# RWKV-6 attention with a channel MLP: how w, k and r of rounds 3 to 7 come to stand with their channels on the partitions

## The chip, the cores and the metric

One NeuronCore of one Trainium2 chip. The time is the device time of one execution in microseconds. The kernel before was run three times: 587.10, 587.24 and 587.42 us, median 587.24. One further execution was recorded by the hardware profiler. It took 585.66 us, of which 583.9 lie between its first and its last instruction (the span); it is a little faster than the median of the others, by 1.6 us.

## What is computed

The reference in two stages. The first is a recurrence over 768 time steps for each of 4 batches and 8 heads, with a head dimension D of 48:

```python
for t in range(S):
    cur = einsum('bhd,bhe->bhde', u * k[t], v[t])
    y[t] = einsum('bhd,bhde->bhe', r[t], state + cur)
    state = w[t][..., None] * state + einsum('bhd,bhe->bhde', k[t], v[t])
```

The second takes the heads side by side as 384 channels, normalizes each step over its channels, scales with `g_ln`, multiplies by `w_ch1` (384 x 1536), takes the positive part, multiplies by `w_ch2` (1536 x 384) and adds the input. Everything is float32.

## The kernel before, in words

**Units and rounds.** A unit is one batch, one half of the sequence (RN = 384 steps) and four heads (two pairs); a round is two units, numbered `g`, so there are 8 rounds of 2 units, `q` = 0 to 15. In the code's main loop (L821) `rnd` is the round whose attention is worked on (`now`), `old` is the one before it and `new` the one after it. While `now` goes through its six levels (`lev` 0 to 5), the MLP of an older round fills TensorE, `old` gets its states and outputs, and the inputs of `new` are loaded and turned.

**The levels.** The attention within chunks of 64 steps is built by doubling: at each level TensorE computes quadrants of scores from k and r (`quads`, L411, into the PSUM tile a_ps), VectorE multiplies k and r by products of w (`grow`, L431) and puts the new scores into the matrix A (`keep`, L448). `grow` of a level comes after `quads` of that level, and `quads` of the next level needs it. After level 5, k is turned back (`ends`, L485, PSUM tile kn_ps), and in levels 0 and 1 of the next round `states` (L504) multiplies it with v (kv) and VectorE runs ten steps of state update; in levels 2 and 3 `outputs` (L560) gives y, which VectorE adds up into x. At level 3 `moments` and `norm` (L597, L607) make the normalized xn on VectorE; at level 4 TensorE turns it (`turned_x`, L623, tile xT_ps); from level 5 on the MLP of that round (`mlp`, L635) runs in steps of three matmuls with 384 columns each (h_ps, then o_ps).

**Turning.** `grow` and `quads` need w, k and r with the channels on the partitions (two heads at 0 and 64) and the steps along the free dimension; in memory the 48 channels of a step lie together. Before, `load` (L122) brings a tensor of a unit with three DMAs of 128 steps x 4 heads x 48 floats into `nat_w`, `nat_k`, `nat_r` (two buffers each, by `q % 2`), steps on the partitions, and `turned` (L306) takes a pair of heads: three TensorE transposes of 128x128 into one PSUM tile (w_ps, k_ps or r_ps) and one ScalarE copy into `wT` or `rkT`. The natural k and r are also what `own_products` (L358, on GpSimd) reads for the term of a step with itself.

**What sets the order.** The compute engines are wrapped so that their instructions stay in the program's order (`InOrder`, L39). In each level the loop collects `tasks` and `fill` (L692) puts them between steps of the MLP. Loads and stores go through the SP queue; its instructions are placed by the framework's scheduler. An instruction on SP waits for the buffer that it writes, and for the completion of the DMA eight places ahead of it, since eight semaphores are used in turn; what stands behind it on SP waits too.

**Weights.** The MLP weights are read early, in 24 pieces of 128 x 768 words, through the tag `raw` of the pool `p4`, which has four buffers; the last piece is used up in round 1's levels.

The part of the loop that the change touches, L866 to L881 of the kernel before, says at which level w, k and r of `new` are loaded and turned: in round 2 w is turned at level 3 and k and r of the two units at levels 4 and 5; in later rounds at levels 1, 2 and 3.

Of the kernel before, what the change touches and what calls it, by code (L numbers as in the profile page):

```python
# [9 lines left out]
F32 = mybir.dt.float32  # L10
# [42 lines left out]
def kernel(  # L53
# [13 lines left out]
    PE, ACT, DVE, POOL, SPO = (  # L67
        InOrder(tc, e) for e in (nc.tensor, nc.scalar, nc.vector, nc.gpsimd, nc.sync)
    )
    SP = nc.sync  # L70

    B, H, S, D = r.shape
    P = 128
    HP = 64
    C = 64
    NH = 4
    NP = NH // 2
    U = H // NH
    TT = 3
    RN = TT * P  # L80
# [3 lines left out]
    W = NK * P  # L84
# [6 lines left out]
    pairs = range(NP)  # L91
# [3 lines left out]
    p1 = ctx.enter_context(tc.tile_pool(name="p1", bufs=1))  # L95
    p2 = ctx.enter_context(tc.tile_pool(name="p2", bufs=2))
    p3 = ctx.enter_context(tc.tile_pool(name="p3", bufs=3))
    p4 = ctx.enter_context(tc.tile_pool(name="p4", bufs=4))
# [8 lines left out]
    units = [(b, f, g) for b, f in rounds for g in range(U)]  # L107
    NU = len(units)
# [24 lines left out]
    def load_rows(nm, q, eng):  # L133

        b, f, g = units[q]
        src = {"w": w, "k": k, "r": r}[nm]
        eng.dma_start(
            out=flat(nm, q)[:, 0 : NH * TT * D].rearrange("p (h x) -> p h x", h=NH),
            in_=src[b, ts(g, NH), ds(f * RN, RN)].rearrange("h (p c) d -> p h (c d)", c=TT),
        )  # L140

    def load_v(q, eng=SP):
        vn[q] = p4.tile([P, TT, NH, D], F32, tag="v", name=f"v{q}")
# [21 lines left out]
    for j in range(2):  # L165
        ACT.dma_start(
            out=sel[ds(HP * j, D), :, j], in_=u.rearrange("(r j) d -> j d r", j=2)[j]
# [23 lines left out]
    for lev in range(NLEV - 1):  # L191
        n = 1 << lev
        m = const.tile([P, C // n, n], I8, name=f"mask2_{lev}")
# [109 lines left out]

    st, carry = {}, {}

    def turned(q, nm, pr):  # L306
        a = st.setdefault(q, {})
        if pr == 0:
            if nm == "w":
                if q % U == 0:  # L310
                    st["w"] = p1.tile([P, U, W], F32, tag="w", name=f"wT{q // U}")
                a["w"] = st["w"][:, q % U]
            elif "rk" not in a:

                rk = a["rk"] = p4.tile([P, 2, W], F32, tag="rkT", name=f"rkT{q}")
                a["r"], a["k"] = rk[:, 0], rk[:, 1]
        ps = ps_t.tile([P, RN], F32, tag="t", name=f"{nm}_ps{q}_{pr}")
        if q < U:


            for c in range(TT):
                for j in (1, 0):
                    at = ((2 * pr + j) * TT + c) * D - HP * j
                    PE.transpose(
                        ps[0 : HP * (j + 1), ts(c, P)],
                        flat(nm, q)[:, ds(at, HP * (j + 1))], ident,
                    )
            (DVE.tensor_copy if q == 0 and pr else ACT.copy)(
                out=a[nm][:, ts(pr, RN)].rearrange("p (m c) -> p m c", c=TT),
                in_=ps.rearrange("p (c m) -> p m c", c=TT),  # L330
            )
            return
        for c in range(TT):
            PE.transpose(
                ps[:, ts(c, P)],
                nat[nm][q % 2][:, c, ts(pr, 2)].rearrange("p j d -> p (j d)"), ident,
            )
        ACT.copy(out=a[nm][:, ts(pr, RN)], in_=ps)
# [371 lines left out]
    def each(f, *ranges):  # L710
        calls = [()]
        for r_ in ranges:
            calls = [c + (x,) for c in calls for x in r_]
        return [lambda c=c: f(*c) for c in calls]
# [106 lines left out]
    for rnd in range(1, NR + 1):  # L821
        old, now, new = units_of(rnd - 1), units_of(rnd), units_of(rnd + 1)
        if rnd == 1:
            old = []
        for lev in range(NLEV):
            slot = (rnd - 1) * NLEV + lev
            if rnd == 2:

                for q in old if lev < 2 else []:
                    (states, outputs)[lev](q)  # L830
                if lev < 2:
                    mlp_step()
            elif old and lev < 2 * U:
                (states if lev < U else outputs)(old[lev % U])
                if lev >= U and now:
                    mlp_step()
            for q in now:
                if slot:
                    quads(q, lev)
            for which in ("rk",) if lev < NLEV - 1 else "kr":  # L840
                for q in now:
                    grow(q, lev, which)
            if now:
                if rnd == 1 and lev == 0:
                    totals(rnd, DVE)
                keep(rnd, lev)
            tasks = []
            if rnd == 1:
                if lev < 2:
                    tasks += each(load, new, "kr"[lev], [SPO])  # L850
                if lev == 2:
                    SPO.dma_start(
                        out=u_bc,
                        in_=bass.AP(
                            tensor=u.tensor, offset=u.offset, ap=[[0, P], [D, H], [1, D]]
                        ),
                    )
                    tasks += each(load_v, now, [SPO])
                if lev == 3:
                    tasks += each(load_vx, now, [SPO])  # L860
                if lev == 1:
                    tasks += each(product_sums, now)
                if lev in (4, 5):
                    own_term(now[lev - 4], POOL)
            if rnd == 2 and lev == 0:
                tasks += each(load_v, now) + each(load, new, "w")  # L866
            if rnd == 2 and lev == 2:
                for q in now:
                    take(DVE, q)
                    tasks += each(load, new[q % U :][:1], "kr")  # L870
            if rnd == 2 and lev in (3, 4):
                tasks += each(own_term, now[lev - 3 :][:1], [POOL])
            if rnd > 2 and lev < 2:
                tasks += each(load, new, ["w", "kr"][lev])
            first = 3 if rnd == 2 else 1
            if rnd > 1 and new and first <= lev < first + 3:
                m = lev - first
                tasks += each(turned, new[m - 1 : m], "kr", pairs) if m else each(
                    turned, new, "w", pairs
                )  # L880
            if rnd == 2:  # L881
                if lev == 0:
                    tasks += each(exchanged, old)
                if lev == 1:
                    tasks += [lambda: moments(1), lambda: norm(1)]
                if lev == 2:
                    tasks += each(turned_x, [1], range(KC))
            elif old and lev < U:
                tasks += each(exchanged, [old[lev]])
            if lev == 3 and rnd > 1:  # L890
                for q in now:
                    load_vx(q)
                for q in new:
                    load_v(q)
                if rnd > 2:
                    moments(rnd - 1)
                    tasks += each(norm, [rnd - 1])
            if lev == 4 and rnd > 2:
                tasks += each(turned_x, [rnd - 1], range(KC))
                tasks += each(own_products, new[:1], [POOL])  # L900
            if lev == NLEV - 1:

                if now:
                    mlp_step()
                if rnd > 2 and new:
                    own_sums(new[0])
                if rnd == 2:
                    tasks += each(own_products, new[:1], [POOL]) + each(own_sums, new[:1])
                if rnd >= 2:
                    tasks += each(own_term, new[:1], [POOL])  # L910
                    tasks += each(own_products, new[1:], [POOL])
                    tasks += each(own_sums, new[1:]) + each(own_term, new[1:], [POOL])
                    if new:
                        tasks += each(totals, [rnd + 1], [POOL])
                if now:
                    tasks = mixed(
                        tasks,
                        each(ends, now, pairs) + each(finish, [2, 2, 4])
                    )
                if rnd == 1:  # L920
                    tasks = [join] * JOINS[lev] + tasks + each(totals, [rnd + 1], [POOL])
            if rnd == 1 and lev < NLEV - 1:

                n = (1, 2, 2, 1, 0, 0)[lev] * NP
                tasks += mixed([begin] * BEGINS[lev], [join] * JOINS[lev], ahead[:n])
                del ahead[:n]
            fill(UNTIL[slot], tasks)
            if lev == (2 if rnd == 2 else 4) and old:
                mlps.append(mlp(rnd - 1))
# [32 lines left out]
```

## Time and profile before

| what | value |
|---|---|
| median of three runs | 587.24 us |
| the profiled execution | 585.66 us |
| its span | 583.9 us |
| mean granted TensorE clock | 0.991 |
| busy: TensorE, VectorE, ScalarE, GpSimd | 572.2, 273.6, 193.8, 90.6 us |
| transposes w_ps, k_ps, r_ps | 108 each |
| DMA, mean over the span | 63 GB/s, 36.52 MB |
| a steady round (290.3 to 358.1 us) | 67.8 us |

A line of a timeline has the start in us, the length in us, the engine, line and operation, the tiles as out<-in, the shape, and a count where like instructions were merged; in square brackets stands the engine's idle time before it and what ended it. All instructions of the wrapped engines have the wrapper's line, L49, so they are told apart by their tiles. A line of windows has the stretch, its length, the busy time of TensorE, its weight loads, VectorE, ScalarE and GpSimd, then the granted clock, the share of time that the 16 DMA engines were busy, and GB/s. A line of DMA issues has the tiles, the count, the size of one, and the median time from issue to landing.

### The profile page before, as it was taken

What the parts mean: (1) busy time and instruction counts of PE and PEld (TensorE: products, weight loads), DVE (VectorE), ACT (ScalarE), POOL (GpSimd) and SP (SyncE); (2) the same over time, 40 slices, a digit from 0 to 9 for tenths busy, and PEclk for the clock granted to TensorE, in tenths of its full rate; (3) what the DMA queues carried; (4) which work ended last, traced back from release to release, by engine and by line L of the source; (5) the groups of instructions that cost most, each with busy time, mean ns of one, the idle gap of its engine ahead of it and who ended that gap; (6) DMA issues with size and microseconds to landing.
All of it is one profiled execution on the core that took longest, in us unless ns stands there. A gap on an engine that the chain in (4) does not pass through costs nothing.

```text
span 583.9 us, 19053 instructions
## 1 busy us (share of the span) xinstructions
PE 572.2 (98%) x8558; PEld 384.1 (66%) x8558; DVE 273.6 (47%) x576; ACT 193.8 (33%) x423; POOL 90.6 (16%) x124
## 2 busy tenths in 40 slices
PE   9999989999999999999999999999999999999997
PEld 7876756666666766666766666666666666666554
DVE  4879898687273634343452543336254531130000
ACT  3577686313442234311432125312331015202200
POOL 6140011104440035000620007000320000000000
PEclk9899899999999999999999999999999999999999
DMA  9938684036315311340204302031000000000000
GB/s 230 203 102 178 175 239 117 16 78 137 64 22 102 72 36 21 68 92 15 57 8 89 65 29 43 2 64 28 15 2 2 16 28 2 2 15 27 0 15 27
DMA packets 114192, 36.52 MB, mean 63 GB/s; under 512 B 104768, under 2 KB 111040, under 8 KB 114112
## 3 DMA queue, kind: packets, MB, share of 16 engines
q1 hardware_dynamic: 112240, 34.72, 26.5%
q8 instruction: 67, 1.10, 0.8%
q10 hardware_dynamic: 1872, 0.59, 0.4%
q14 instruction: 13, 0.11, 0.1%
HBM read 28.51 MB, written 4.72 MB: 57 GB/s over the span
## 4 chain that ended last, share of the span: by engine, by line
PE 91%; ACT 4%; DVE 2%; issue 1%; DMA 1%; ACTq 0%; DVEq 0%
PE o_ps L49 32%; PE h_ps L49 30%; PE a_ps L49 11%; PE y L49 4%; PE kv L49 2%; PE k_ps L49 2%; PE r_ps L49 2%; PE w_ps L49 2%; PE kn_ps L49 2%; PE xT_ps L49 1%; ACT rest L49 1%; PE own_ps L49 1%; PE idle L49 1%; ACT rkT L49 1%; ACT w_sb L49 1%
## 5 line engine op out<-in xcount | busy, mean ns | idle before, releaser
L49 PE MATMUL o_ps<-w_sb,h 128*128 128x384 f32 x576 | 199.0, 490 | 0.9 <-ACT h L49 0.9
L49 PE MATMUL h_ps<-xT,w_sb 128*128 128x384 f32 x576 | 198.7, 493 | 0.0
L49 PEld LDWEIGHTS h_ps<-xT,w_sb 128*128 128x128 f32 x576 | 105.7, 191 | 63.1 <-issue 0.9
L49 PEld LDWEIGHTS o_ps<-w_sb,h 128*128 128x128 f32 x576 | 104.4, 190 | 62.0 <-ACT h L49 1.8
L49 DVE TENSOR_TENSOR rkT<-rkT,tot 128x768 f32<-128x768 f32 (+1 forms) x96 | 76.7, 841 | 38.9 <-issue 26.0
L49 ACT ACTIVATE h<-h_ps 128x384 f32<-128x384 f32 x96 | 46.8, 488 | 144.7 <-PE h_ps L49 144.6
L49 PEld LDWEIGHTS a_ps<-rkT 48*64 48x64 f32 x4608 | 73.2, 136 | 20.8 <-issue 13.4
L49 PE MATMUL a_ps<-rkT 48*64 48x32 f32 x4608 | 78.4, 221 | 0.1
L49 DVE TENSOR_TENSOR o<-o_ps,x 128x384 f32<-128x384 f32 x24 | 13.4, 557 | 121.9 <-PE o_ps L49 121.8
L49 POOL TENSOR_TENSOR vo<-v,own 128x576 f32<-128x576 f32 x16 | 19.2, 1203 | 288.7 <-DVE own L49 251.9
L49 DVE SCALAR_TENSOR_TENSOR s<-s,decay,kv 128x48 f32<-128x48 f32 x160 | 29.3, 259 | 33.9 <-PE kv L49 33.9
L49 DVE TENSOR_TENSOR x<-y,vo 128x288 f32<-128x288 f32 x32 | 13.2, 453 | 53.8 <-PE y L49 53.7
L49 DVE COPY_PREDICATED A<-mask,a_ps 128x768 f32<-128x768 int8 x32 | 38.3, 1197 | 0.0
L49 ACT COPY rkT<-k_ps 128x384 f32<-128x384 f32 x31 | 13.9, 478 | 57.3 <-PE k_ps L49 57.1
L49 ACT ACTIVATE xT<-xT_ps,g_sb 128x384 f32<-128x384 f32 x24 | 13.6, 579 | 54.0 <-PE xT_ps L49 54.0
L49 ACT COPY rkT<-r_ps 128x384 f32<-128x384 f32 x31 | 14.2, 478 | 24.2 <-PE r_ps L49 24.1
L49 DVE TENSOR_SCALAR w_sb<-w_sb 128x384 f32<-128x384 f32 (+1 forms) x48 | 19.5, 406 | 0.8
L49 ACT ACTIVATE rstd<-mv,eps 128x3 f32<-128x3 f32 x8 | 2.4, 296 | 49.2 <-DVE mv L49 49.1
L49 DVE TENSOR_REDUCE own<-rk 128x12 f32<-128x576 f32 x12 | 9.0, 750 | 20.7 <-POOL rk L49 20.6
L49 ACT COPY wT<-w_ps 128x384 f32<-128x384 f32 x31 | 14.0, 478 | 14.1 <-PE w_ps L49 14.1
L49 PE MATMUL r_ps<-ident,nat_r 128*128 128x128 f32 x108 | 16.2, 279 | 2.2 <-ACT rkT L49 2.1
L49 DVE TENSOR_TENSOR rkT<-rkT,wT 128x768 f32<-128x768 f32 x16 | 17.5, 1131 | 0.9 <-PE a_ps L49 0.8
(76 smaller groups left out, 517.9 us busy)
## 6 DMA issues: line engine op xcount, KB each, us to landing
raw<-in_moe_w_ch_dram SPq DMA_DIRECT2D x24, 384.0 KB, 4.3
v<-in_v_dram SPq DMA_DIRECT2D x48, 96.0 KB, 3.3
out_dram<-o SPq DMA_DIRECT2D x24, 192.0 KB, 1.9
nat_w<-in_w_dram SPq DMA_DIRECT2D x42, 96.0 KB, 2.9
nat_r<-in_r_dram SPq DMA_DIRECT2D x42, 96.0 KB, 2.8
nat_k<-in_k_dram SPq DMA_DIRECT2D x42, 96.0 KB, 3.1
vx<-v SPq DMA_DIRECT2D x28, 72.0 KB, 2.3
nat_r<-in_r_dram ACTq DMA_DIRECT2D x2, 288.0 KB, 4.9
```

Of the source, the lines that this page charges most:

```text
L49: return lambda *args, **kw: self.tc.keep_in_program_order(f(*args, **kw))
```

## The change

For the units of rounds 3 to 7, ten units, w, k and r are brought in a second form and turned by VectorE. A new `stage` loads a pair of heads: for each head j, 64 partitions receive runs of the tensor, partition 32 e + t the 560 floats that start at step 12 t, channel 32 e (e is 0 or 1, t is 0 to 31). A run spans 12 steps. The buffers are those of the tag `raw`. A new `squares` then turns the 12 blocks of 32 channels of a whole 128-partition tile with one VectorE instruction in squares of 32x32, straight into `wT` or `rkT`, and takes the place of `turned` for these units. The blocks with e = 1 hold the channels 32 to 47 and then 16 floats of the next step, which land on partitions that nothing reads. The last run of the tensor is cut into two DMAs.

`stage` is called one level before `squares`: in round 2 at levels 2, 3 and 4, later at levels 0, 1 and 2. `load` of w for these units falls away; `load` of k and r stays, at level 1. The core of the diff:

```diff
+    SQ = 32
+    NS = RN // SQ
+    ROW = (NS - 1) * D + SQ
+    staged = {}
+
+    def stage(q, nm, pr, eng=SP):
+        b, f, g = units[q]
+        src = {"w": w, "k": k, "r": r}[nm]
+        t = p4.tile([P, WC, 2], F32, tag="raw", name=f"{nm}_runs{q}_{pr}")
+        t = staged[q, nm, pr] = t.rearrange("p n two -> p (n two)")[:, 0 : NS * D]
+        for j in range(2):
+            first = src.offset + ((b * H + g * NH + 2 * pr + j) * S + f * RN) * D
+            if (q, pr, j) == (NU - 1, NP - 1, 1):
+
+                POOL.memset(t[P - SQ :, NS * D - SQ :], 0.0)
+                both = [(e, 1, ROW - e * (ROW - NS * D + SQ)) for e in range(2)]
+            else:
+                both = [(0, 2, ROW)]
+            for e, many, n in both:
+                eng.dma_start(
+                    out=t[ds(HP * j + SQ * e, SQ * many), 0:n],
+                    in_=bass.AP(
+                        tensor=src.tensor, offset=first + SQ * e,
+                        ap=[[SQ, many], [NS * D, SQ], [1, n]],
+                    ),
+                )
...
+    def squares(q, nm, pr):
+        a = st[q] if pr else turned_to(q, nm)
+        DVE.transpose(
+            out=a[nm][:, ts(pr, RN)].rearrange("p (t s) -> p s t", s=NS),
+            in_=staged.pop((q, nm, pr)).rearrange("p (s d) -> p s d", s=NS)[..., 0:SQ],
+        )
...
-                tasks += each(load_v, now) + each(load, new, "w")
+                tasks += each(load_v, now)
...
-            if rnd > 2 and lev < 2:
-                tasks += each(load, new, ["w", "kr"][lev])
+            if rnd > 2 and lev == 1:
+                tasks += each(load, new, ["kr"])
             first = 3 if rnd == 2 else 1
-            if rnd > 1 and new and first <= lev < first + 3:
+            if rnd > 1 and new and first - 1 <= lev < first + 3:
                 m = lev - first
-                tasks += each(turned, new[m - 1 : m], "kr", pairs) if m else each(
-                    turned, new, "w", pairs
-                )
+                turns = [(new, "w"), (new[:1], "kr"), (new[1:], "kr")]
+                if m >= 0:
+                    tasks += each(squares, *turns[m], pairs)
+                if m < 2:
+                    tasks += each(stage, *turns[m + 1], pairs)
```

`turned_to` holds the lines of `turned` that make the tiles `wT` and `rkT`; `turned` calls it now. Rounds 0 to 2 are turned as before.

More of the change, by code (lines that the diff above doesn't have):

```diff
@@ L304, with turned_to @@
     st, carry = {}, {}
-    def turned(q, nm, pr):
[L307 to L316, printed above, removed]
+    def turned_to(q, nm):
+        a = st.setdefault(q, {})
+        if nm == "w":
+            if q % U == 0:
+                st["w"] = p1.tile([P, U, W], F32, tag="w", name=f"wT{q // U}")
+            a["w"] = st["w"][:, q % U]
+        elif "rk" not in a:
+            rk = a["rk"] = p4.tile([P, 2, W], F32, tag="rkT", name=f"rkT{q}")
+            a["r"], a["k"] = rk[:, 0], rk[:, 1]
+        return a
+    def squares(q, nm, pr):
[4 more added lines that the diff above has]
+        )
+    def turned(q, nm, pr):
+        a = st[q] if pr else turned_to(q, nm)
         ps = ps_t.tile([P, RN], F32, tag="t", name=f"{nm}_ps{q}_{pr}")
```

## The prediction

> **What bounds the kernel now.** I read the page's busy shares and chain first, then one round in time order on TensorE and on VectorE, then the DMA rows.
>
> ```profile
> PE 572.2 (98%) x8558; PEld 384.1 (66%) x8558; DVE 273.6 (47%) x576; ACT 193.8 (33%) x423; POOL 90.6 (16%) x124
> PE 91%; ACT 4%; DVE 2%; issue 1%; DMA 1%; ACTq 0%; DVEq 0%
> PE o_ps L49 32%; PE h_ps L49 30%; PE a_ps L49 11%; PE y L49 4%; PE kv L49 2%; PE k_ps L49 2%; PE r_ps L49 2%; PE w_ps L49 2%; PE kn_ps L49 2%; PE xT_ps L49 1%; ACT rest L49 1%; PE own_ps L49 1%; PE idle L49 1%; ACT rkT L49 1%; ACT w_sb L49 1%
> ```
>
> TensorE is 98% busy and the chain that ends last runs on it for 91%: whatever leaves its stream is gained, as long as no other engine or transfer becomes late. Now level 1 of a steady round on TensorE, then the same place on VectorE:
>
> ```profile
> 368.27 2.20 PE L49 MATMUL h_ps<-xT,w_sb 128*128 128x384 f32 x6
> 370.31 0.49 PE L49 MATMUL w_ps<-ident,nat_w 128*128 128x128 f32 x3
> 370.64 2.10 PE L49 MATMUL h_ps<-xT,w_sb 128*128 128x384 f32 x6
> 372.57 0.82 PE L49 MATMUL w_ps<-ident,nat_w 128*128 128x128 f32 x6
> 373.23 2.10 PE L49 MATMUL h_ps<-xT,w_sb 128*128 128x384 f32 x6
> ```
> ```profile
> 368.78 1.82 DVE L49 TENSOR_TENSOR rkT<-rkT,tot 128x768 f32<-128x768 f32 x2
> 370.52 1.86 DVE L49 COPY_PREDICATED A<-mask,a_ps 128x768 f32<-128x768 int8 x1
> ```
>
> Read starts, not durations: three transposes hold the stream from 370.31 to 370.64, 0.33 us, or 0.11 us each, though each is shown longer because matmuls overlap. VectorE is done with this level at 372.4 and has room. The third place is the end of level 3, where VectorE's xn feeds TensorE's next transposes:
>
> ```profile
> 328.64 0.97 DVE L49 COPY_PREDICATED A<-mask,a_ps 128x768 f32<-128x768 int8 x1
> 332.01 1.26 DVE L49 TENSOR_SCALAR xn<-x,mv,rstd 128x384 f32<-128x384 f32 x3
> ```
> ```profile
> 336.21 0.55 PE L49 MATMUL xT_ps<-ident,xn 128*128 128x128 f32 x3
> ```
>
> xn is ready at 333.3 and wanted at 336.2: 2.9 us of slack. Last the transfers:
>
> ```profile
> 80.00:84.00 4.00, 4.00 (x76) 2.85 (x70) 4.00 (x4) 3.61 (x9) 1.27 (x1) 1.00 1.04 379
> 290.30:358.10 67.80, 67.80 (x1053) 45.63 (x1049) 29.46 (x63) 19.75 (x44) 12.76 (x13) 1.00 0.24 50
> ```
> ```profile
> nat_w<-in_w_dram SPq DMA_DIRECT2D x42, 96.0 KB, 2.9
> ```
>
> Each window ends in granted clock, DMA share and GB/s. With all 16 DMA engines full (share 1.04) they moved 379 GB/s of long rows: 23.7 GB/s for one engine. A steady round of 67.8 us has them busy 24%, 16 us each.
>
> [...] No transpose on VectorE is in the trace. [...]
>
> **Part 1, transposes leave TensorE.** `new` in rounds 2 to 6 is ten units; 3 tensors x 2 pairs x 3 transposes each: 180. At 0.11 us (the chain agrees: w_ps, k_ps and r_ps are 5.9% of 583.9 us for 324, 0.106 each) that is 19.5 us, 3.9 a round. ACT loses 60 copies of 478 ns, 29 us; it is 33% busy, so nothing.
>
> **Part 2, squares come to VectorE.** 60 instructions of 384 elements. Nearest rows: a 128x384 two-input operation, 555 ns, a one-input one, 477. I take 0.56, four per level 2.2 us, bounds 0.48 and 1.1 (as if half as fast). At levels 1 and 2 this lies in idle time. At level 3 they stand between the moments and xn: xn's end moves from 333.3 to 335.4, while TensorE without its 12 transposes wants it at 334.9: under 1 us a round, 3 at 1.1 us each.
>
> **Part 3, the loads.** Leaving: nat_w, 6 DMAs a round. Coming: 24 a round, each 64 rows of 560 floats, 143 KB. In the changed program the source of each is 2 x 32 x 560 and the destination 64 x 560[...]. (Only the three cut at the tensor's end are 32 against 32.) An engine then moves 71.7 KB:[...] 3.0 by the trace's; I take d = 2.9. Were all 16 used it would be 0.4 us, and the change would be free of this: that is the other end of this cost. All 24 sit on the same two engines: 70 us a round, plus about 14 of other traffic (16 less nat_w), against a round of 68. And they come in chained batches, since the four "raw" buffers hold one batch of 8: w, then k and r of the first unit, then of the second. A batch starts only when VectorE has turned the one before, so nothing can run ahead.
>
> Steady round, marks of before. The w squares start at S = 372.4. Batch 2 is issued from S+0.6; with 2.4 us fixed latency (2.9 to land a nat_w, less 0.5 of transfer) and 8 x 2.9 it lands by S+26.2, while VectorE reaches its squares at about S+11.4. VectorE stalls there; queued behind on it are the o and x sums and grow of level 3. On SP, v and then vx follow batch 2; vx waits for v, which is behind it on the rings: 3 us more. Batch 3 (issued now, 2.4 + 23.2) lands at S+54.8. Behind its squares stand the reciprocal and xn: 0.6 + 1.5, xn at S+56.9. TensorE waits there, in front of xT. Before, xT came at S+31.6 (404.0). So **+25.3 us** a round, the saving of 3.9 already inside. This holds for rounds 4, 5 and 6: 76, less about 6 for the last round's loads that use 16 engines: 70.
>
> Round 2 turns at levels 3, 4, 5. The w squares end at 141.4 (loaded long before). Batch 2 lands until 165, its last square ends 165.6, behind it grow of level 5, which TensorE needs for kn: 166.8 where it was 153.5. Batch 3 follows on the rings until 188.7; its last square ends 189.3, and the second unit's first a_ps waits for it, 163.3 before: **+26**. Round 3: S is 176.6 + 26 = 202.7. Its w loads were behind batch 3 and land until 211.7; SP then has 12 nat loads, some waiting for GpSimd's rk, ahead of batch 2, which I let start at 219. It lands by 245, batch 3 by 269, xn 271.3 against xT at 202.6: **+69** so far. Sum: 69 + 70 = **+139**. The profiled execution of 585.66 (span 583.9) becomes 724.7; the median stands 1.6 above it: **726**.
>
> **Rivals.** (a) All 16 engines carry each load[...]. Then the batch of 8 lands 6 us after its issue, inside the 11.4, and only parts 1 and 2 count: 587.2 - 19.5 + 2 = 570, faster. It turns at d of about 1.05 us ((11.4 - 0.6 - 2.4)/8): five to six engines. For it: nothing in the trace excludes it.[...] (b) Two engines, but they pipeline better or the SP waits cost nothing, so only their throughput counts[...]. With four engines (d 1.5) each of some 11 batches is 8 x 1.4 = 11.2 us shorter: 726 - 123 = 603. (c) VectorE becomes the bound: at 1.7 us a square, xn is 6.8 - 2.9 + 1.3 = 5.2 us late in five rounds, 594.[...]
>
> **How the numbers follow.** Likeliest, k = 2 with the chain as told: 0.74; its own range 675 to 780 (d of 2.5 or 3.3 over some 100 loads in series is -40 or +40, the SP waits +-12). Rival (a) 0.15; (b) and what lies between 0.08; (c) 0.01; beyond 780, 0.02. Leaving out (a) and the extremes gives 615 to 795. Faster by over 0.2%, about what a measurement of this kernel can tell from no change: 0.15; within: 0.01; slower: 0.84.
>
> **What would show it.** Right: w_runs, k_runs and r_runs land 8 to 25 us after issue (alone about 5), DMA share a round stays low (24 loads on 2 engines of 16 are some 13 points of it) while VectorE's waits are led by rkT on DMA k_runs and r_runs, and TensorE idles some 25 us a round before xT_ps, released by DVE xn; TensorE's share falls to near 75%. Part 1 alone is right if w_ps, k_ps and r_ps count 48 each and the steps around them follow 0.33 us sooner per three. Wrong: staged loads landing in 3 us each, TensorE at 98% in a round of 64 us; or StreamTranspose far from 0.56 us.

## The result, and the profile after

The changed kernel takes 744.75 us (median of four runs, 742.75 to 746.18), the kernel before 587.33 beside it: a ratio of 1.267, 95% interval 1.264 to 1.271. The profiled execution took 745.29 us, with a span of 742.8 and a mean granted clock of 0.874. The forecast was 726, in a range of 615 to 795. First the busy shares and the chain of the changed kernel's page, to set beside those of before:

```profile
PE 575.3 (77%) x8378; PEld 379.4 (51%) x8378; DVE 321.5 (43%) x636; ACT 168.9 (23%) x363; POOL 95.1 (13%) x127
PE 47%; DMA 22%; issue 10%; SPq 8%; DVE 7%; ACT 3%; POOL 2%; DVEq 0%; POOLq 0%; ACTq 0%
PE h_ps L49 17%; DMA r_runs<-in_r_dram 16%; PE o_ps L49 16%; PE a_ps L49 5%; DMA k_runs<-in_k_dram 4%; SPq L164 4%; SPq L125 3%; DVE rkT L49 3%; PE y L49 2%; DMA nat_r<-in_r_dram 2%; POOL rk L49 1%; PE kv L49 1%; DVE A L49 1%; PE xT_ps L49 1%; PE kn_ps L49 1%
```

Read the counts first. TensorE runs 180 matmuls fewer (8558 before) and VectorE 60 instructions more (576): the change does what it says. Then the shares: TensorE has no less busy time than before, only a longer span around it. The chain says what fills that: transfers of r_runs and k_runs are 20% of it, and two entries of the SP queue, L164 (the new loads) and L125 (k and r in their natural form), another 7%. The list of waits of the changed kernel (engine and tile, what it waited for, us in all, times, the longest) names who stands still:

```profile
DVE rkT L49 <- DMA r_runs<-in_r_dram: 98.7, 20, 5.2
PE xT_ps L49 <- DVE xn L49: 89.3, 4, 24.9
DVE rkT L49 <- DMA k_runs<-in_k_dram: 74.6, 16, 10.8
PE a_ps L49 <- DVE rkT L49: 46.9, 7, 21.2
```

VectorE waits 173 us for the two tensors, and TensorE, behind VectorE, 89 us in four places, each just ahead of the transposes of xn. (PEld waits beside it, for the same xn.) VectorE's timeline in a steady round of the changed kernel shows how one comes from the other:

```profile
412.60 2.94 DVE L49 STREAM_TRANSPOSE wT<-w_runs 128x384 f32<-128x384 f32 x4
...
427.99 0.87 DVE L49 STREAM_TRANSPOSE rkT<-k_runs 128x384 f32<-128x384 f32 x1 [3.43 <-DMA k_runs<-in_k_dram]
434.07 0.87 DVE L49 STREAM_TRANSPOSE rkT<-r_runs 128x384 f32<-128x384 f32 x1 [5.21 <-DMA r_runs<-in_r_dram]
439.95 0.85 DVE L49 STREAM_TRANSPOSE rkT<-r_runs 128x384 f32<-128x384 f32 x1 [5.02 <-DMA r_runs<-in_r_dram]
...
468.65 0.84 DVE L49 STREAM_TRANSPOSE rkT<-r_runs 128x384 f32<-128x384 f32 x1 [5.09 <-DMA r_runs<-in_r_dram]
469.56 1.26 DVE L49 TENSOR_SCALAR xn<-x,mv,rstd 128x384 f32<-128x384 f32 x3
```

The squares of w cost no wait in this round. Those of k and r come one by one: from the second of a batch on they stand 5.8 to 6.1 us apart, most of them after a wait of some 5 us. A square needs a pair of heads, which is two DMAs: about 2.93 us for each of 143 KB. Behind the last one stands xn, and behind xn, on TensorE's timeline of the changed kernel in the round ahead of this one:

```profile
374.46 1.26 PE L49 MATMUL xT_ps<-ident,xn 128*128 128x128 f32 x3 [24.91 <-DVE xn L49]
375.51 3.36 PE L49 MATMUL o_ps<-w_sb,h 128*128 128x384 f32 x6
379.04 2.10 PE L49 MATMUL o_ps<-w_sb,h 128*128 128x384 f32 x6
```

The transposes stand 24.9 us idle, where before they followed with no wait. The second line shows something more: right after the stall six matmuls take 3.36 us, and the next six the usual 2.10. The windows of the changed kernel over the stall and the 5.5 us after it show a lower clock there (the last three numbers are the granted clock, the DMA share and GB/s):

```profile
346.00:374.50 28.50, 2.59 (x97) 2.46 (x97) 8.24 (x17) 0.30 (x1) 0.00 (x0) 0.52 0.21 64
374.50:380.00 5.50, 5.50 (x15) 3.19 (x16) 3.77 (x6) 1.16 (x2) 0.00 (x0) 0.68 0.19 43
```

The clock was 0.52 in the stall and 0.68 after it, and the DMA engines as a whole were busy only 0.21 of the time while VectorE waited for them. A low share beside long waits fits a few full engines among many idle ones; the experiments test that.

### The profile page after: what moved, and what is told of

Read it like the earlier page. It is cut to its first block, busy times and chain, and to the rows that moved or that the text cites. A ratio compares the mean times of both kernels' runs of the same rounds, so it can differ in the third digit from the quotient of the medians.

```text
span 742.8 us, 18836 instructions
## 1 busy us (share of the span) xinstructions
PE 575.3 (77%) x8378; PEld 379.4 (51%) x8378; DVE 321.5 (43%) x636; ACT 168.9 (23%) x363; POOL 95.1 (13%) x127
## 4 chain that ended last, share of the span: by engine, by line
PE 47%; DMA 22%; issue 10%; SPq 8%; DVE 7%; ACT 3%; POOL 2%; DVEq 0%; POOLq 0%; ACTq 0%
PE h_ps L49 17%; DMA r_runs<-in_r_dram 16%; PE o_ps L49 16%; PE a_ps L49 5%; DMA k_runs<-in_k_dram 4%; SPq L164 4%; SPq L125 3%; DVE rkT L49 3%; PE y L49 2%; DMA nat_r<-in_r_dram 2%; POOL rk L49 1%; PE kv L49 1%; DVE A L49 1%; PE xT_ps L49 1%; PE kn_ps L49 1%
## 5 line engine op out<-in xcount | busy, mean ns | idle before, releaser
L49 PE MATMUL o_ps<-w_sb,h 128*128 128x384 f32 x576 | 205.2, 506 | 1.0 <-ACT h L49 1.0
L49 PEld LDWEIGHTS o_ps<-w_sb,h 128*128 128x128 f32 x576 | 109.3, 197 | 69.5 <-issue 5.9
L49 PE MATMUL a_ps<-rkT 48*64 48x32 f32 x4608 | 83.5, 227 | 48.3 <-DVE rkT L49 46.9
L49 PEld LDWEIGHTS a_ps<-rkT 48*64 48x64 f32 x4608 | 77.7, 143 | 69.3 <-DVE rkT L49 51.4
L49 PE MATMUL xT_ps<-ident,xn 128*128 128x128 f32 x72 | 15.5, 322 | 89.8 <-DVE xn L49 89.3
L49 PEld LDWEIGHTS xT_ps<-ident,xn 128*128 128x128 f32 x72 | 10.3, 157 | 98.3 <-DVE xn L49 91.8
L49 DVE STREAM_TRANSPOSE rkT<-r_runs 128x384 f32<-128x384 f32 x20 | 17.0, 848 | 98.7 <-DMA r_runs<-in_r_dram 98.7
L49 DVE STREAM_TRANSPOSE rkT<-k_runs 128x384 f32<-128x384 f32 x20 | 17.1, 853 | 76.4 <-DMA k_runs<-in_k_dram 74.6
L49 PE MATMUL kn_ps<-ident,rkT 128*128 128x128 f32 x96 | 14.8, 291 | 18.6 <-DVE rkT L49 17.7
L49 PEld LDWEIGHTS kn_ps<-ident,rkT 128*128 128x128 f32 x96 | 11.8, 148 | 24.5 <-DVE rkT L49 18.3
```

Of the source, the lines that this page charges most:

```text
L49: return lambda *args, **kw: self.tc.keep_in_program_order(f(*args, **kw))
```

## The experiments

The theory is that of the prediction: a staged load goes over 2 of the 16 DMA engines, since the outermost count of its source is 2; it is slow for that, and because k and r are issued only when w's buffers are free, the slowness lies on the path. The two engines (k = 2 there, k being the number of engines that carry a load) were my assumption; no trace of before shows them. The rivals: it is the amount of data or the number of loads, the size of one load, or VectorE's new work. Runs of the kernel before beside these: 587.96 us for the kernels with the rows in another order, with TensorE kept busy and with the squares side by side, 586.85 for the other four.

**Each load cut in two.** Every staged load becomes two DMAs of 32 rows, with 32 as its outermost count:

```diff
-                    out=t[ds(HP * j + SQ * e, SQ * many), 0:n],
+                    out=t[ds(HP * j + SQ * e, SQ), 0:n],
...
-                        ap=[[SQ, many], [NS * D, SQ], [1, n]],
+                        ap=[[NS * D, SQ], [1, n]],
```

> The changed kernel with every staged load cut into two DMAs of 32 rows (one per block of channels)[...]. Same bytes, same rows of 560 floats, same buffers, same squares; twice as many DMAs (48 a round). Theory (two engines carried each load of 64 rows, 2.93 us each, in batches of eight): each DMA is spread over 16 engines, the waits of VectorE on k_runs and r_runs (173 us) fall below 15 us, and what stays is the gain of 19.5 us of transposes less xn that is late behind four squares of 0.85 us: 336.7 against 334.9, 1.8 us in four rounds, 7 us. 576 us, between 568 and 584. Rival (it is the shape of the runs, the chain through four buffers, or the number of DMAs, not the engines): 700 us or more, since all of these stay or grow.

Measured: 580.8 us (577.89 to 583.25), 0.988 of before (0.983 to 0.992). VectorE's waits for r_runs fell from 98.7 us to 5.3 and for k_runs from 74.6 to 1.3:

```profile
DVE rkT L49 <- DMA r_runs<-in_r_dram: 5.3, 4, 2.2
DVE rkT L49 <- DMA k_runs<-in_k_dram: 1.3, 2, 0.8
```

The same bytes, through the same four buffers, turned by the same squares, are 164 us quicker than in the changed kernel. But this edit doubles the number of DMAs too, so it does not yet say whether the spread over engines or the number of DMAs did it.

**The same loads, rows in another order.** One number pair is exchanged, nothing else; one DMA of 64 rows stays one DMA of 64 rows:

```diff
-                        ap=[[SQ, many], [NS * D, SQ], [1, n]],
+                        ap=[[NS * D, SQ], [SQ, many], [1, n]],
```

> The changed kernel with the rows of each staged load in another order: still one DMA of 64 rows of 2240 bytes, from the same bytes to the same partitions, but the source is walked as 32 pairs instead of as 2 groups of 32 (the rows land in another order, so w, k and r of rounds 3 to 7 are computed with other steps than the reference's). The number of DMAs, of rows and of bytes is that of the changed kernel, so this tells the order of the rows apart from all three. Theory (the outermost count of the source, 2, decides how many DMA engines carry a load): with 32 outermost the loads spread, a pair of them lands in 2 to 3 us instead of 5.9, the waits for r_runs and k_runs fall from 173 us to under 15, and the time is that of the loads cut in two, about 580 us (572 to 592). Rival 1 (64 rows of over 2 KB in one DMA, or the raw buffers, are slow in themselves, in whatever order): nothing changes, 738 to 750 us. Rival 2 (it was the number of DMAs in flight that helped when the loads were cut in two): 738 to 750 us too.

Measured: 577.25 us (575.8 to 580.1), 0.983 of before (0.976 to 0.990). Rivals 1 and 2 fall. The number, size and bytes of the loads are those of the changed kernel, and the 167 us are gone. The waits of this kernel, against 98.7 and 89.3 us above (no wait of VectorE for k_runs is listed at all):

```profile
DVE rkT L49 <- DMA r_runs<-in_r_dram: 3.6, 4, 1.4
PE xT_ps L49 <- DVE xn L49: 2.0, 1, 2.0
```

The SP queue shows it from the other side. In both kernels the first four loads of a batch are issued in 2.5 us. The next four, first of the changed kernel and then of this one:

```profile
416.09 10.91 SPq L164 DMA_DIRECT2D r_runs<-in_r_dram  x4
```
```profile
309.46 2.47 SPq L164 DMA_DIRECT2D r_runs<-in_r_dram  x4
```

SP needs 10.9 us for four in the changed kernel, 2.60 to 2.77 us each and so about the time of one load. This is not the wait for the DMA eight places ahead that is told above of SP (in the trace of before 243 of SP's 255 DMAs raise the semaphore of the one eight places ahead): for each of these four, that DMA had landed by 410.4. In the records the issue of each ends 0.5 to 1.0 us before the load four places ahead has landed; why it takes so long was not shown. The three loads of v, next on SP, are held up too: their issue takes 9.39 us, against 2.61 with the rows interleaved. There, four loads are issued in 2.47 us, and the page of this kernel gives a landing time of 2.8 us for k_runs and 2.9 for r_runs, latency included. The rate of a slow load fits two engines: 143 KB in 2.93 us is 49 GB/s, 24.5 for each of the two, beside 23.7 for one of sixteen full ones in the trace of before.

The packets show the number two as well. The two kernels' counts of DMA packets, first of the changed kernel and then of this one:

```profile
DMA packets 106363, 50.75 MB, mean 68 GB/s; under 512 B 89258, under 2 KB 95530, under 8 KB 106282
DMA packets 108001, 50.76 MB, mean 88 GB/s; under 512 B 90896, under 2 KB 97168, under 8 KB 107920
```

The difference, 1638, lies in packets under 512 B alone, and in the records of the trace all of it is packets of 4 bytes: 14 fewer for each of the 117 loads of 64 rows. In the trace of before SP's queue has 4080 of them, 16 for each of its 255 DMAs; in the changed kernel it has 3930, which is 16 for each of 231 DMAs and 2 for each of these 117. The same records hold start and length of each of the 7584 packets of 2240 bytes. In the changed kernel at least one of them is under way for 358 us, and for 310 of these it is exactly two; with the rows interleaved it is ten or more for 58 of 93 us. So a slow load goes over two engines, as far as packets and rate can tell, and in this kernel the order of the source's dimensions decides it. That the new order also reads memory in another sequence is no way out: the loads cut in two keep the sequence of each block of channels and are about as quick (580.8 us).

**Only w, or only r, in the slow form.** In both kernels 8 of a round's 24 loads keep the slow form and the others are cut in two:

```diff
-                both = [(0, 2, ROW)]
+                both = [(0, 2, ROW)] if nm == "w" else [(0, 1, ROW), (1, 1, ROW)]
```

> Only the loads of w keep the 64-row form on two engines (8 of 24 a round); k and r are cut into 32 rows. Theory (what hurts is the wait of a batch that is issued one level ahead; w is issued nearly a whole round ahead): w still takes 23 us to land and nobody waits for it; within 5 us of the run with 32 rows everywhere, 574 to 582. Rival (the load on the two engines as such, by its amount): a third of the loss of 169 us between that run and the changed kernel, about 630.

> Only the loads of r keep the 64-row form on two engines, again 8 of 24 a round, but in two batches of four that are issued one level ahead. Theory: the first batch lands by S+19, and level 2 has room for that (grow of level 3 can't start before about S+20); the second lands by about S+40 and xn ends at S+42 where TensorE comes at S+27.7: some 12 us a round more than with 32 rows everywhere in rounds 3 to 6, and about 15 us in round 2: 640 us, between 618 and 662, with the waits of VectorE on r_runs leading and those on k_runs under 15 us. Rival (amount alone): the same as with w on two engines.

Measured: only w slow 589.29 us (1.0045 of before, 1.0022 to 1.0067), only r slow 647.96 us (1.101, 1.096 to 1.107). The waits, first of the kernel with only w slow, then of that with only r slow:

```profile
PE xT_ps L49 <- DVE xn L49: 6.4, 1, 6.4
DVE wT L49 <- DMA w_runs<-in_w_dram: 4.3, 1, 4.3
```
```profile
DVE rkT L49 <- DMA r_runs<-in_r_dram: 75.2, 19, 5.9
PE xT_ps L49 <- DVE xn L49: 42.5, 4, 12.0
```

The same number of slow loads of the same size costs 8.5 us (against all cut in two) in one place and 67 in the other. For w the next batch is issued at level 0, 36 us ahead of its squares in a steady round of the changed kernel (471.64 to 507.95), and eight loads of 2.93 us fit in there. For r it is issued when w's squares free a buffer, and VectorE wants it 11 us later: TensorE stands up to 12.0 us a round. That rules out the amount as the cause. The 8.5 us are more than the 5 that my theory allowed, and 589.29 lies outside its 574 to 582. The trace puts 7.6 of them in one place, round 3: its xn starts at 213.14, against 205.52 with all loads cut in two. There w was issued from 158.24 on, behind round 2's k and r and 20 us ahead of its squares (178.05), where eight loads of 2.93 us take 23; VectorE waited the 4.3 us above for it, and then for k and r behind it.

**The squares behind xn.** With the loads fast, something still kept the kernel above the 568 that 180 transposes promise. VectorE's timelines at level 3, first with the loads cut in two, then with one change of order on top, where from round 3 on the squares of level 3 stand behind the normalization:

```diff
-                if m >= 0:
-                    tasks += each(squares, *turns[m], pairs)
+                behind = each(squares, *turns[m], pairs) if m >= 0 else []
+                if m < 2 or rnd == 2:
+                    tasks += behind
+                    behind = []
...
                     tasks += each(norm, [rnd - 1])
+                    tasks += behind if new else []
```

```profile
330.92 1.55 DVE L49 STREAM_TRANSPOSE rkT<-k_runs 128x384 f32<-128x384 f32 x2
332.31 1.52 DVE L49 STREAM_TRANSPOSE rkT<-r_runs 128x384 f32<-128x384 f32 x2
333.68 0.15 DVE L49 RECIPROCAL rstd<-rstd 128x3 f32<-128x3 f32 x1
333.89 1.26 DVE L49 TENSOR_SCALAR xn<-x,mv,rstd 128x384 f32<-128x384 f32 x3
```
```profile
324.18 0.18 DVE L49 RECIPROCAL rstd<-rstd 128x3 f32<-128x3 f32 x1 [0.36 <-ACT rstd L49]
324.39 1.26 DVE L49 TENSOR_SCALAR xn<-x,mv,rstd 128x384 f32<-128x384 f32 x3
325.56 1.54 DVE L49 STREAM_TRANSPOSE rkT<-k_runs 128x384 f32<-128x384 f32 x2
326.94 1.53 DVE L49 STREAM_TRANSPOSE rkT<-r_runs 128x384 f32<-128x384 f32 x2
```

> As the one before, and from round 3 on the four squares of level 3 stand behind the reciprocal and xn in VectorE's order. Theory (part 2's only cost on the path is xn behind the squares): the rest of the 7 us comes back, 569 us, between 565 and 573, and TensorE waits on xn for under 2 us in all. Rival (squares hurt through VectorE's load as a whole[...]): the same as the run before within 1.5 us.

Measured: 573.13 us (572.25 to 573.6), 0.975 of before (0.972 to 0.978). It is 7.7 us quicker than with the loads cut in two alone, the longest wait for xn falls from 2.2 us to 0.5, and it beats both kernels. In the first block xn stands behind 2.8 us of squares; in the second it comes first.

The order does not explain all of the 7.7 us, though, and what it explains is not spread evenly. The two traces part ahead of the first place that the edit touches: in round 3 both kernels idle some 2.2 us before a_ps, after which 96 a_ps and 18 o_ps matmuls take 2.78 and 7.87 us with the loads cut in two, and 1.60 and 6.07 in this kernel. That makes 2.3 us of the 7.7 and is no doing of the edit. Then come the transposes of xn in round 3 and the six matmuls behind them, first with the loads cut in two, then in this kernel:

```profile
206.06 1.81 PE L49 MATMUL xT_ps<-ident,xn 128*128 128x128 f32 x6 [2.10 <-DVE xn L49]
207.67 3.45 PE L49 MATMUL o_ps<-w_sb,h 128*128 128x384 f32 x6
```
```profile
201.58 0.87 PE L49 MATMUL xT_ps<-ident,xn 128*128 128x128 f32 x6
202.29 2.10 PE L49 MATMUL o_ps<-w_sb,h 128*128 128x384 f32 x6
```

The stall there costs 2.1 us and the slower stretch after it as much again; each later round gains 0.4. So the order of the squares is worth some 5.4 us in this pair of traces, 4.4 of it from that one stall.

The time is 4 us above what I expected, just outside 565 to 573. The trace says where: a steady round is 63.95 us (transposes of xn at 263.60 and 327.55), against 67.8 before, so 3.9 a round are gained in full from round 4 on. But the first transposes of xn, ahead of any square, come at 129.74 instead of 126.70; and the stretch from there to those of round 3, in which two rounds' inputs are turned, is 4.0 us shorter and not 7.8. In it some squares still waited for their loads. Why the start is 3 us later was not tried.

**TensorE kept busy in the stall.** The changed kernel, with stand-in matmuls ahead of the transposes of xn:

```diff
             if lev == 4 and rnd > 2:
+                if new:
+                    warm(96, "t")
```

> The changed kernel with 96 small matmuls on a scratch tile (some 21 us) in TensorE's queue ahead of the transposes of xn in rounds 3 to 7, where TensorE otherwise stands idle for 25 us a round: the wait stays, the engine only stays busy in it. It tests the term by which the prediction was short in every round (38.1 us from the transposes to the next squares of w, against 36.2 before, with a granted clock of 0.52 in the stall and 0.68 just after it). Theory (the lower clock after the stall costs about 2 us a round): the six o_ps matmuls after the transposes take 2.1 us instead of 3.4, and the time falls by 1.5 to 2.5 us in each of four or five rounds, to 733 to 740 us. Rival (the 2 us come from VectorE's and GpSimd's work and not from the clock): the time stays at 743 to 747 us. If the warm matmuls run past the arrival of xn, up to 5 us a round are added: 745 to 765.

Measured: 742.9 us (740.5 to 743.75), 1.266 of before (1.258 to 1.273). Against the changed kernel (1.264 to 1.271) the intervals overlap: as a time, this run shows no gain, and the 733 to 740 that I expected are missed. In the trace the rounds differ. The windows of this kernel over the stand-in matmuls and the 6 us after them, in two rounds:

```profile
346.50:371.70 25.20, 22.32 (x69) 12.78 (x65) 4.63 (x11) 0.30 (x1) 0.00 (x0) 0.95 0.21 64
371.70:377.50 5.80, 5.74 (x16) 3.21 (x17) 3.68 (x6) 1.16 (x2) 0.00 (x0) 0.71 0.18 45
442.80:468.00 25.20, 23.62 (x69) 13.32 (x65) 5.01 (x12) 0.30 (x1) 0.00 (x0) 0.90 0.20 64
468.00:474.00 6.00, 5.92 (x23) 3.66 (x24) 3.75 (x6) 1.56 (x3) 0.00 (x0) 1.00 0.19 46
```

In the second pair (round 5; TensorE idled the last 1.6 us) the clock is 1.00 after the stall, and from the transposes of xn to the next squares of w it takes 36.4 us, as before (36.2), instead of the 37.9 of the changed kernel there. In the first pair (round 4; idle for the last 2.9 us) the clock was 0.71 afterwards all the same, and the stretch took 38.4 (38.1 in the changed kernel). In round 3 it took 34.0, as before (34.2), against 37.3. In the last of these rounds, round 6, the stand-ins outlasted the arrival of xn (557.1) and held the transposes until 562.0, which gave some 4 us back; from there to the next transposes of xn it took 65.9 us, as before (66.0), against 68.6 in the changed kernel. So in three of four rounds the stretch after the stall was as long as before once the clock was up, 1.4 to 3.3 us shorter than in the changed kernel. That supports the clock as the cause of this term; it rests on one trace of each kernel, and the time of the whole does not show it.

**The squares written side by side.** On top of the loads cut in two:

```diff
-            out=a[nm][:, ts(pr, RN)].rearrange("p (t s) -> p s t", s=NS),
+            out=a[nm][:, ts(pr, RN)].rearrange("p (s t) -> p s t", s=NS),
```

> The loads cut in two, with the squares written side by side instead of 48 bytes apart (the 32 by 32 squares come out in another order of steps, so w, k and r of rounds 3 to 7 are computed with other steps than the reference's). It tests why a StreamTranspose of 128x384 took 0.85 us where the prediction took 0.56. Theory (the stride of the output costs it): 0.52 to 0.60 us each, and 60 of them free some 17 us of VectorE, of which at most 2 to 5 us show in the time: 575 to 581 us. Rival (the operation itself takes some 2.1 ns an element): 0.83 to 0.87 us as before, and 578 to 583 us.

Measured, in a single execution: 576.41 us, too little for a statement on the time. The groups of the squares of k, with their mean in ns after the busy time, first with the loads cut in two, then in this kernel:

```profile
L49 DVE STREAM_TRANSPOSE rkT<-k_runs 128x384 f32<-128x384 f32 x20 | 15.8, 849 | 1.4 <-DMA k_runs<-in_k_dram 1.3
```
```profile
L49 DVE STREAM_TRANSPOSE rkT<-k_runs 128x384 f32<-128x384 f32 x20 | 10.6, 558 | 3.0 <-DMA k_runs<-in_k_dram 2.9
```

849 ns becomes 558 by the output's layout alone. 0.56 us is also what a two-input operation of that shape takes in the trace of before (555 ns). Writing each 4-byte element 48 bytes from the last costs half as much again.

## Why the prediction was right, step by step

| delay against before, us | predicted | measured |
|---|---|---|
| transposes of xn in round 3 | 69 | 77.1 (279.63 against 202.52) |
| added by round 4 | 25.3 | 29.0 (374.46 against 268.39) |
| added by round 5 | 25.3 | 27.8 (470.09 against 336.21) |
| added by round 6 | 19.4 | 22.9 (560.80 against 404.02) |
| from there to the end | 0 | 2.1 |
| sum | 139 | 158.9 (span 742.8 against 583.9) |

The mechanism was right and the delay 20 us short, 139 against 159. Every row of the table is short, so no error hid another.

**Part 1** holds: 180 matmuls left, and where nothing waits a round is 3.9 us shorter (63.95 against 67.8, with xn first), the predicted figure.

**Part 2** was mis-sized: 0.56 us a square is right for a dense output and 0.85 for this one. In the changed kernel this hides in the waits for loads. In the kernel with fast loads it is what stands ahead of xn. It can matter there in four rounds, 3 to 6, and is worth some 5.4 us: 0.4 a round in rounds 5 and 6, within the "under 1 us" of the prediction, but over 4 in round 3 with the slower stretch behind it, where the prediction had no slower matmuls after a stall (six o_ps in 3.45 us instead of 2.10).

**Part 3**, the engines and the chain of batches, holds. d was taken as 2.9 us and is 2.93. In the round with S = 412.6, batch 2's last square starts at S + 27.4 (landing predicted for S + 26.2), batch 3's at S + 56.1 (S + 54.8), the transposes of xn at S + 57.5 (xn at S + 56.9). What was short in rounds 4 to 6, 9.7 us, falls into three parts. Two thirds, 6.4, are a term that the sum did not have: from the transposes of rounds 3, 4 and 5 to the next S it took 37.3, 38.1 and 37.9 us where before it took 34.2, 36.4 and 36.2. (I had taken every round of before as 67.8 us; from round 3 to round 4 it was 65.9, and the difference lies in this stretch.) The kernel with stand-in matmuls points to the granted clock behind it in two of the three rounds. The stretch from S to the transposes was 0.6 us over in rounds 4 and 5 each, with d and the latency a little over. And the last round's loads saved 4 us and not the 6 that I took off. Of the end, 2.6 us arise by the next transposes and 0.5 are won back later; the clock was 0.52 for 5.2 us after the last stall, and with the stand-ins these 2.6 are gone.

**Rounds 2 and 3** came 8.1 us later than predicted. In round 2 the squares of w began at 142.66 instead of 139.1: VectorE was 2.4 us late already (xn at 128.42, before 126.00), and the grow ahead of the squares took 3.75 us, against 2.53 in the trace of before. From the issue of the next sixteen loads (143.54) to the start of the last square (194.12) it took 50.6 us; the prediction had 49 to the last landing. In round 3 the squares of w waited 4.2 us for their loads, and k and r were issued at 226.25, where I had let them start at 219. The step "+69 so far" failed in its size by these, not in its mechanism.

**The rivals.** (a), all sixteen engines, would give 570 by the prediction; the runs in which the loads do spread gave 577 and 581, and 573 with xn first: the size of that case was near, but the changed kernel's loads had two packets under way at a time. (b), the throughput of two engines alone, misses the waits: with only r slow, a third of the loads already costs 67 us more than with none. (c) fell with the squares at 0.85 us.

## What to carry to other kernels

Look at the outermost count of a DMA's source before its bytes: the same 64 rows in the order 32 x 2 instead of 2 x 32 took this kernel from 745 to 577 us. That order puts the rows on other partitions, so that kernel computes something else; two DMAs of 32 rows keep the rows in place, at 581 us. And then ask how far ahead a load is issued: eight slow loads a round were nearly free where they were issued 36 us ahead, and cost 67 us in all where a buffer became free only 11 us ahead. When a step is moved onto an engine that also feeds the critical one, put it behind the instruction that is waited for; that was worth some 5 us here, most of it in the one round in which the critical engine really had to wait.

## What the runs showed of the hardware

- A square transpose of VectorE, 128x384 in float32, takes 0.54 to 0.56 us with a dense output and 0.85 us when it writes each element 48 bytes from the last.
- After some 25 us with TensorE almost idle (busy 2.59 of 28.5 us) the clock granted was 0.52, and 0.68 in the 5.5 us that followed; six matmuls took 3.36 us instead of 2.10. With TensorE kept busy in the stall (22.32 of 25.2 us in one round) the clock after it was 1.00 in three rounds and 0.71 in one.
- Slower matmuls can follow a short stall too, but need not: after 2.2 us without work 96 a_ps and 18 o_ps matmuls took 2.78 and 7.87 us with the loads cut in two, and 1.60 and 6.07 us after 2.3 us in the same place of the kernel with xn first.
- A load of 64 rows with 2 outermost in its source had two packets under way at a time (for 310 of 358 us), and with 32 outermost ten or more (for 58 of 93 us). Four DMAs of the second kind are issued by SP in 2.5 us; four of the first, behind four others, hold SP for 10.9 us.
